# Second products of an attention tile grouped with the scores of the tile two further on

## The chip, the cores and the metric

The program runs on one core of a Trainium2 chip. The metric is the device time of one execution in microseconds (us); each figure in the table below is a whole execution, and the number to be predicted is the median over repeated runs. The engines are PE (matrix products, with PEld for its weight loads), DVE (elementwise), ACT (activations and copies), POOL and SP. In this kernel POOL and SP mostly start DMA transfers, each from a queue that is worked through in order.

## What is computed

Chunked attention, then two feed-forward layers, all in float32:

```python
# q, k, v: batch 8, heads 8, sequence 576, head size 64; chunks of 64
scores = scale * q_c @ k_c.T            # inside each chunk only
attn = softmax(scores)
x = (attn @ v_c)                        # -> 4608 tokens x 512
h = x @ w_in                            # 512 -> 2048
g = maximum(h, 0) + log1p(exp(-abs(h))) # softplus
x = g @ w_out                           # 2048 -> 512
h = maximum(maximum(x @ w1, x @ w2), x @ w3)   # 512 -> 768
out = h @ w_out2                        # 768 -> 512
```

## The kernel before, in words

Tokens are cut into 9 blocks of 512 (`NB`). The attention of a block is 4 tiles (two heads each), 36 tiles in all (`NTILE`). Weights are made of two float32r parts, so a product is three passes. The first three blocks (`NP`) go through `mlp1`: 48 steps, each with 12 matmuls into `ph` and 12 into `acc`. The other six blocks use `UnitA`, seven products a unit in the manner of Strassen, with `mlp1_out`; their weight forms are made in `weightsa`, written to DRAM (`wac`, `wae`) and read back by POOL in `againa`, up to nine slots ahead (`ringa`). The second layer (`Unit2`, `Unit`, `mlp2_out`) follows after some 900 us.

Tiles 0 to 7 are computed by `attention_first`. Tiles 8 to 35 go through `attention(t)`, whose steps are: SP loads q and k (`load_32`, four loads for each piece of the tile), POOL loads v into `rv`, of which there is one buffer (`load_v`); DVE transposes q and k into a slot `QK`; PE computes the scores in the PSUM buffer `aps`, also one; DVE and ACT make the softmax in `p`; DVE transposes it into the slot `PT` in blocks of 32; SP writes it to DRAM (`pd`, L667) and reads it back in four pieces that finish the transposition (L672). PE then multiplies it with v, and `to_x` copies the product out as the layer's input. The products with v of one tile and the scores of another share one `aps` buffer and one PE instruction group, `products` (32 matmuls of 64x64 each). Which two tiles share a group is decided by the list `before`: in the kernel before, group t holds the scores of tile t and the products of tile t-1.

Nobody writes the order of the work by hand. Every piece is an `op` with the engines that may do it, an assumed cost, an assumed extra latency (`lat`) and a due time (`due`). `Plan.order` simulates a list schedule with these assumed numbers, earliest due time first, and hands out buffers and slots as it goes; the order that comes out is each engine's program. On the chip each engine then runs its own list in that order and waits where something isn't there. A step is 6 us in the plan's due times (`STEP`). An operation without a due time gets one by counting back from the operations that need it, their cost and `lat` included.

Slots (46 tiles of 128x2x512) are shared by kind: `w` 32, `x` 8, `z` 4, `qh` 1, `vh` 1. `vh` first holds the signed identities of `conv1`. Raw weights (`conv`) go to `z` or `w`, the last ones to `z` alone; `QK` takes `qh` or `z`; `PT` takes `vh` or `z`.

Of the kernel before, what the change touches and what calls it, by code (L numbers as in the profile page):

```python
# [179 lines left out]
def tile_kernel(ctx: ExitStack, tc: tile.TileContext, q, k, v, w_in, w_out, w1, w2, w3, wo2, out):  # L180
# [71 lines left out]
    def slot(*kinds, shape=[P, 2, TB], dt=F32R):  # L252
        return Buf(*kinds, fresh=lambda i: slot_at(i, shape, dt))
# [26 lines left out]
    NP = 3  # L280
# [179 lines left out]
    def loads(fns, buf, key, move, alloc=(), engs="S", after=(), due=None):  # L460
        fns = list(fns)
        if alloc:
            op({engs: 0.0}, lambda e: None, alloc=alloc, after=after)
        for n, fn in enumerate(fns):
            op(
                {e: 0.5 if due is not None else 0.65 for e in engs},
                lambda e, fn=fn: fn({"A": nc.scalar, "S": nc.sync, "G": nc.gpsimd}[e].dma_start),
                w=[(buf, (key, n))],
                after=after,
                lat=4.0 if due is None else 1.8,  # L470
                move=move / len(fns),
                due=due,
            )
# [140 lines left out]
    def attention(t, after=()):  # L614

        if t < NTILE:
            Rq, Rk, Rv = Buf("rq"), Buf("rk"), Buf("rv")
            QK = slot("qh", "z", dt=F32)
            qT, kT = half(QK, 0), half(QK, 1)
            loads(load_32(t, q, lambda: Rq.t), Rq, "q", 2.2, [Rq], after=after)  # L620
            loads(load_32(t, k, lambda: Rk.t), Rk, "k", 2.2, [Rk], after=after)
            loads(load_v(t, lambda: Rv.t, 0), Rv, "v", 1.6, [Rv], "G", after)
            op({"D": 0.69}, lambda e: nc.vector.transpose(qT(), Rq.t), r=[Rq], w=[(QK, "q")], alloc=[QK])
            op({"D": 0.69}, lambda e: nc.vector.transpose(kT(), Rk.t), r=[Rk], w=[(QK, "k")])
        G = Buf("aps")
        old = before.pop() if before else None

        def products(e):
            if old:
                v4 = old[1].t.rearrange("p (c e d) -> p c e d", e=2, d=D)  # L630
                p4 = old[2].t[:, 1].rearrange("p (a u i) -> p u a i", a=2, i=32)
                for c in range(HP):
                    for r, k in four:
                        at = slice(TB // 2 + c * CH, TB // 2 + (c + 1) * CH)
                        square(G.t[:, :, at], v4[:, c, k], p4[:, k * HP + c], r, k)
            if t < NTILE:
                scores(G, qT, kT)

        parts = [(G, "v")] * (old is not None) + [(G, "s")] * (t < NTILE)
        op(  # L640
            {"P": 0.5 * len(parts) + 0.4},
            products,
            r=([old[1]] + [(old[2], n) for n in range(4)] if old else []) + ([(QK, "q"), (QK, "k")] if t < NTILE else []),
            w=parts,
            alloc=[G],
            after=last_t[-1:],
            due=T0 + STEP * (4 * (t - 1 - HP) + (2.25 if t <= NP * HP else -0.75)),
        )
        if old:

            def view(z, flat):
                if flat:
                    return z.rearrange("p (r f) -> p r f", r=2)
                return z[:, :, TB // 2:]

            to_x(old[0], G, view)
        if t == NTILE:
            return
        pbuf = Buf("p")
        softmax(G, pbuf)  # L660
        PT = slot("vh", "z", dt=F32)
        pt, pT = half(PT, 0), half(PT, 1)
        op({"D": 0.69}, lambda e: nc.vector.transpose(
            pt().rearrange("p (b u i) -> p b u i", b=2, i=32), pbuf.t.rearrange("p (u b i) -> p b u i", b=2, i=32)
        ), r=[pbuf], w=[(PT, "pt")], alloc=[PT])
        pd = Buf("pd")
        op({"S": 0.48}, lambda e: nc.sync.dma_start(out=pd.t, in_=pt()), r=[(PT, "pt")], w=[pd], alloc=[pd], lat=3.0)  # L667
        for n in range(4):
            c, b = divmod(n, 2)
            op(  # L670
                {"S": 0.48},
                lambda e, n=n, c=c, b=b: nc.sync.dma_start(  # L672
                    out=pT()[n * 32:(n + 1) * 32, :].rearrange("j (a f) -> j a f", a=2),
                    in_=pd.t[c * CH:(c + 1) * CH, b * (TB // 2):(b + 1) * (TB // 2)].rearrange("(a j) f -> j a f", a=2),
                ),
                r=[pd],
                w=[(PT, n)],
                lat=4.0,
            )
        before.append((t, Rv, PT))  # L680

# [298 lines left out]

    STAYA = (6, 7)
    EARLY = 4
    GATE = 5
    wa = {}
    began = []

# [419 lines left out]
    def strassen():  # L1406

        groups = [(b, b + 1) for b in range(0, NB - 1, 2)] + [(NB - 1,)]
        units = [("a", b, n) for b in range(NP, NB) for n in range(NJ // 2)]
        units += [("b", i, n) for i in range(len(groups)) for n in range(3 * NJ2 // 2)]  # L1410
        old, outs, side, ready, earlies = None, [], [], [], 0
        for kind, i, n in units + [("", None, 0)]:
            new = None
            if kind == "a":
                at = NJ * i + 2 * n
                t = HP + at // HP
                clock[0] = T0 + STEP * at
                if at % HP == 0 and t <= NTILE:
                    attention(t, [first_loads[11]])
                if n == 0:  # L1420
                    splita(i)
                new = UnitA(i, n, old)
                begin = new.p1()
                if n in (1, 2, 3, 4, 6) and earlies < 4 * NJ2:
                    early(earlies, T0 + STEP * (at + EARLY), [begin])
                    earlies += 1
                if i == NB - 1:
                    mark[n] = begin
            if kind == "b":
                if (i, n) == (0, 0):  # L1430
                    clock[0] = T1
                    for m in range(3 * NJ2 // 2):
                        ready = [weights2(m)]
                    split2(groups[0], [mark[4]])
                new = Unit2(groups[i], n) if i + 1 < len(groups) else Unit(NB - 1, n)
                begin = new.p1()
                if n == 4 and i + 1 < len(groups):
                    if i + 2 < len(groups):
                        split2(groups[i + 1], ready + [begin])
                    else:  # L1440
                        split(NB - 1, [begin])
            if old:
                old.p5()
                old.p4()
            if new:
                new.p6()
            if kind == "a" and outs:
                out_of, *which = outs.pop(0)
                in_line("h", out_of(*which))
            if old:  # L1450
                old.p3()
            if new:
                new.p2()
                new.p7()

            if isinstance(old, UnitA):
                outs += [(mlp1_out, old.b, 2 * old.n + f) for f in (1, 0)]
                pops, least = (1 if kind == "a" else 2), 1
            else:
                pops, least = 2 if len(outs) > 3 else 1, i is None or i + 1 == len(groups)  # L1460
            for _ in range(pops):
                if len(outs) > least:
                    out_of, *which = outs.pop(0)
                    o = out_of(*which)
                    if out_of is mlp1_out:
                        in_line("h", o)
            if isinstance(old, (Unit, Unit2)) and old.i == 2:
                for h, b in enumerate(old.b if isinstance(old, Unit2) else (NB - 1,)):
                    (side if h else outs).extend([(mlp2_out, b, 2 * old.jp + f) for f in range(2)])
                if old.jp == NJ2 // 2 - 1:  # L1470
                    outs, side = outs + side, []
            old = new
        for out_of, *which in outs:
            out_of(*which)
# [24 lines left out]
    for n, (b, j, first, last) in enumerate(steps):  # L1499
        if n >= NJ and n % (NJ // HP) == 0:  # L1500
            t = HP + n // (NJ // HP)
            attention(t, [first_loads[min(t, 11)]])
        h = mlp1(b, j, first, last)
        if b == NP - 1 and j % 2 == 0:
            weightsa(j // 2, [before_last], lead)
        if (b, j) == (1, NJ // 2):
            lead = h
        before_last = h if j % 2 == 0 else before_last
# [38 lines left out]
```

## Time and profile before

| | us |
|---|---|
| runs: median of 3 | 1456.22 |
| runs: lowest, highest | 1453.78, 1457.23 |
| profiled execution, its own time | 1451.92 |
| its span, first to last instruction | 1449.8 |
| mean granted PE clock | 0.987 of full |
| PE busy, share of the span | 97% |
| DVE, ACT, POOL busy | 61%, 35%, 18% |

The profiled execution is one run. Its span starts with the program's first instruction; 2.1 us of its time lie outside. PE's busy time counts matmuls that run at either clock, so a stretch at half clock looks busy. The time line of this program: until 72 us the first tiles and weights, until about 332 us the steps of `mlp1`, until about 900 us the units of `UnitA`, and then the second layer.

### The profile page before, as it was taken

Reading aid. Unit: us, or ns where it says so; the run is one execution under the profiler, and the core shown is the slowest. Engines: PE = TensorE matmul, PEld = TensorE weight load, DVE = VectorE, ACT = ScalarE, POOL = GpSimd, SP = SyncE. Lnnn points to the kernel's source line nnn. Section 1 sums busy time; section 2 is a strip of 40 time slices with the busy share of each in tenths; the row PEclk is TensorE's granted clock in tenths of the full one; section 3 lists DMA queues with packets and bytes.
Section 4 is the critical chain, followed back from the end, with each engine's and each line's share of the span. In section 5 each row is a group of like instructions: output and inputs, shape, how many; then the busy total and the mean of one; then the engine's idle time right before and its main releaser. Section 6 shows DMA issues by size and latency. Waiting matters only on the chain.

```text
span 1449.8 us, 25676 instructions
## 1 busy us (share of the span) xinstructions
PE 1399.2 (97%) x9994; PEld 1200.1 (83%) x9994; DVE 881.6 (61%) x1678; ACT 509.6 (35%) x998; POOL 267.1 (18%) x471
## 2 busy tenths in 40 slices
PE   5999999999899897999998999999999999999998
PEld 4788788888798786888998998888888888888897
DVE  8978866766585575665765457766435444644423
ACT  4533222434344242243343445434213322322212
POOL 1000121332223232323222010211011111101300
PEclk9999999999999998999999999999999999999999
DMA  8554366687867859767567275855344533625720
GB/s 256 172 144 108 110 195 191 181 257 226 263 179 213 263 158 272 216 186 239 178 242 256 101 232 207 302 196 188 119 165 140 206 134 98 232 74 177 294 106 30
DMA packets 232473, 271.99 MB, mean 188 GB/s; under 512 B 143456, under 2 KB 163296, under 8 KB 232352
## 3 DMA queue, kind: packets, MB, share of 16 engines
q0 software_dynamic: 49472, 169.64, 33.4%
q1 hardware_dynamic: 182064, 99.93, 24.5%
q8 instruction: 79, 1.29, 0.4%
q10 hardware_dynamic: 816, 0.79, 0.2%
q14 instruction: 42, 0.34, 0.1%
HBM read 208.14 MB, written 62.13 MB: 186 GB/s over the span
## 4 chain that ended last, share of the span: by engine, by line
PE 85%; DMA 7%; issue 3%; DVE 3%; POOL 1%; SPq 1%; ACT 1%; DVEq 0%; ACTq 0%; POOLq 0%
PE ph L1279 14%; PE acc L1176 13%; PE ph L1102 12%; PE acc L1387 10%; PE one L1279 10%; PE acc L737 9%; PE ph L717 9%; DMA s<-pd 3%; PE aps L486 2%; DMA pd<-s 2%; PE ph L970 2%; PE one L970 1%; PE acc L486 1%; PE ph L388 1%; POOL rv L453 1%
## 5 line engine op out<-in xcount | busy, mean ns | idle before, releaser
L1176 PE MATMUL acc<-g,s 128*128 128x512 f32 x1152 | 284.4, 396 | 0.0
L1102 PEld LDWEIGHTS ph<-s,s 128*128 128x128 f32 x2016 | 256.3, 193 | 10.2 <-ACT tmp L1124 2.1
L1102 PE MATMUL ph<-s,s 128*128 128x256 f32 x2016 | 261.4, 285 | 1.4 <-ACT tmp L1124 1.2
L1176 PEld LDWEIGHTS acc<-g,s 128*128 128x128 f32 x1152 | 213.5, 191 | 41.8
L266 ACT COPY tmp<-ph 128x256 f32<-128x256 f32 (+1 forms) x271 | 123.2, 454 | 349.4 <-PE ph L1279 218.7
L1279 PE MATMUL ph<-s,s 128*128 128x512 f32 x864 | 212.6, 389 | 0.0
L273 DVE TENSOR_TENSOR tmp<-one,tmp 128x512 f32<-128x512 f32 (+1 forms) x123 | 77.8, 632 | 211.8 <-PE one L1279 173.2
L1279 PEld LDWEIGHTS ph<-s,s 128*128 128x128 f32 x864 | 162.2, 188 | 33.6
L453 POOL DMA_DIRECT2D rv<-in_v_dram x152 | 93.6, 623 | 359.8 <-PE aps L486 306.9
L1279 PE MATMUL one<-s,s 128*128 128x512 f32 x648 | 158.8, 389 | 0.0
L273 DVE TENSOR_TENSOR g<-tmp,g 128x512 fp32r<-128x512 f32 x168 | 115.0, 686 | 65.8 <-ACT g L266 65.2
L273 DVE TENSOR_TENSOR tmp<-ph,tmp 128x256 f32<-128x256 f32 (+1 forms) x172 | 76.5, 455 | 114.8 <-PE ph L1102 114.6
L1279 PEld LDWEIGHTS one<-s,s 128*128 128x128 f32 x648 | 121.5, 188 | 25.0
L737 PE MATMUL acc<-g,s 128*128 128x512 f32 x576 | 140.2, 392 | 0.0
L717 PE MATMUL ph<-s,s 128*128 128x512 f32 x576 | 139.4, 392 | 0.0
L717 PEld LDWEIGHTS ph<-s,s 128*128 128x128 f32 x576 | 109.0, 190 | 23.0
L737 PEld LDWEIGHTS acc<-g,s 128*128 128x128 f32 x576 | 107.1, 188 | 23.0 <-DVE g L273 0.3
L844 POOL DMA_DIRECT2D s<-w2c x96 | 51.1, 533 | 354.2 <-PE one L1279 130.5
L266 ACT CAST g<-tmp 128x512 fp32r<-128x512 f32 x163 | 101.6, 623 | 39.4 <-PE acc L737 18.6
L1124 ACT ACTIVATE tmp<-tmp 128x256 f32<-128x256 f32 x96 | 50.4, 525 | 148.6 <-DVE tmp L273 148.6
L266 ACT CAST s<-tmp 128x512 fp32r<-128x512 f32 (+1 forms) x122 | 72.0, 601 | 62.9 <-DVE tmp L273 42.0
L1039 POOL DMA_DIRECT2D s<-wac x108 | 59.2, 549 | 166.0 <-PE ph L1102 139.6
(134 smaller groups left out, 1511.8 us busy)
## 6 DMA issues: line engine op xcount, KB each, us to landing
s<-wac POOLq DMA_DIRECT2D x108, 512.0 KB, 5.5
s<-w2c POOLq DMA_DIRECT2D x96, 512.0 KB, 4.6
w2c<-s POOLq DMA_DIRECT2D x24, 512.0 KB, 4.2
wac<-s POOLq DMA_DIRECT2D x18, 512.0 KB, 4.3
x2d<-tmp SPq DMA_DIRECT2D x36, 256.0 KB, 3.7
s<-wae POOLq DMA_DIRECT2D x18, 512.0 KB, 6.5
s<-in_moe_w_dram POOLq DMA_DIRECT2D x18, 512.0 KB, 5.1
s<-in_moe_w_in_dram SPq DMA_DIRECT2D x16, 512.0 KB, 4.6
```

Source lines behind the costliest of these rows:

```text
L266: nc.scalar.copy(dst(), src())
L273: return op({"D": 0.69 * n}, lambda e: nc.vector.tensor_tensor(dst(), a(), b(), f), r=r, w=w, **kw)
L453: dma(out=dst().rearrange("p (c e d) -> p c e d", e=2, d=D)[half * CH:(half + 1) * CH, lo:lo + mine, h, :], in_=v[b, t % HP * 2 + h].rearr ...
L717: nc.tensor.matmul(ph.t, w[:, wi, kk * P:(kk + 1) * P], x[kk].t[:, xi], start=(kk == 0 and wi == 0 and xi == 0), stop=(kk == KD - 1 and wi ...
L737: nc.tensor.matmul(acc[m // 2].t[:, m % 2], w[:, wi, m * P:(m + 1) * P], g.t[:, gi, :], start=(first and wi == 0 and gi == 0), stop=(last ...
L844: lambda e, k=k, z=z, w=w: nc.gpsimd.dma_start(out=z.t[:, :, w].bitcast(F32), in_=(w2e[n // 2] if k == 3 else w2c[n][k])[:, :, w]),
L1039: lambda e, k=k: nc.gpsimd.dma_start(out=new[k].t.bitcast(F32), in_=wac[n][k] if k < 3 else wae[n // 2]),
L1102: nc.tensor.matmul(z.t[:, half * HT:(half + 1) * HT], ws.t[:, wi, col + kk * P:col + (kk + 1) * P], x.t[:, xi, kk * HT:(kk + 1) * HT], sta ...
L1124: in_line("y", op({"A": n}, lambda e: nc.scalar.activation(to(), src(), AF.Softplus), r=r, w=w))
L1176: nc.tensor.matmul(acc[m // 2].t[:, m % 2], w.t[:, wi, m * P:(m + 1) * P], g.t[:, gi, :], start=(first and wi == 0 and gi == 0), stop=(las ...
L1279: nc.tensor.matmul(dst(), ws.t[:, wi, col + kk * P:col + (kk + 1) * P], x[kk].t[:, xi], start=(first and kk == 0 and wi == 0 and xi == 0), ...
L1387: nc.tensor.matmul(acc[t // 2].t[:, t % 2], g.t[:, gi, t * P:(t + 1) * P], wo.t[:, wi], start=(j == 0 and wi == 0 and gi == 0), stop=(j == ...
```

## The change

Group t now holds the scores of tile t and the products of tile t-2. So that products come out at the same place of the loops, every tile's `attention` call stands one tile earlier (two calls at the first place), and there are two last groups without scores. The due time of the groups is given by a new formula, the assumed latencies of the loads, of the write to `pd` and of the reads back are raised, `PT` may also take a slot of kind `w`, and the reads back of `wac` are let go one `weightsa` earlier (`GATE`).

```diff
@@ loads
-                lat=4.0 if due is None else 1.8,
+                lat=5.0 if due is None else 1.8,
@@ attention
-        old = before.pop() if before else None
+        old = before.pop(0) if len(before) == 2 or t >= NTILE else None
...
-            due=T0 + STEP * (4 * (t - 1 - HP) + (2.25 if t <= NP * HP else -0.75)),
+            due=T0 + STEP * (13.0 + 3.56 * (t - 2 * HP) if t <= 4 * HP else 4 * t - 23.0),
...
-        if t == NTILE:
+        if t >= NTILE:
             return
...
-        PT = slot("vh", "z", dt=F32)
+        PT = slot("vh", "z", "w", dt=F32)
...
-        op({"S": 0.48}, lambda e: nc.sync.dma_start(out=pd.t, in_=pt()), r=[(PT, "pt")], w=[pd], alloc=[pd], lat=3.0)
+        op({"S": 0.48}, lambda e: nc.sync.dma_start(out=pd.t, in_=pt()), r=[(PT, "pt")], w=[pd], alloc=[pd], lat=8.0)
...
-                lat=4.0,
+                lat=8.0,
@@ strassen and the steps of mlp1
-    GATE = 5
+    GATE = 4
...
-                t = HP + at // HP
+                t = HP + at // HP + 1
...
-                if at % HP == 0 and t <= NTILE:
+                if at % HP == 0 and t <= NTILE + 1:
...
-            attention(t, [first_loads[min(t, 11)]])
+            for t in ((t, t + 1) if n == NJ else (t + 1,)):
+                attention(t, [first_loads[min(t, 11)]])
```

## Rows read from the trace of the kernel before

**Rows 1.** The page: span; busy time and share of PE and others.

```profile
span 1449.8 us, 25676 instructions
PE 1399.2 (97%) x9994; PEld 1200.1 (83%) x9994; DVE 881.6 (61%) x1678; ACT 509.6 (35%) x998; POOL 267.1 (18%) x471
```

**Rows 2.** PE's waits, 126 to 800 us: total, times, longest.

```profile
PE aps L486 <- DMA s<-pd: 27.0, 12, 8.0
PE ph L388 <- DVE s L345: 1.5, 1, 1.5
```

**Rows 3.** A window: length, busy time by engine, PE clock, DMA share, GB/s.

```profile
800.00:1365.00 565.00, 565.00 (x2701) 476.45 (x2700) 302.74 (x509) 193.98 (x364) 77.76 (x145) 1.00 0.49 174
```

**Rows 4.** Windows of PE alone at half clock: two of five, and their sum.

```profile
391.23:398.05 6.82, 5.49 (x71) 0.50 0.69 191
...
572.13:582.37 10.24, 4.35 (x69) 0.50 0.86 237
...
sum 27.29, PE 20.07; mean PE 4.01
```

**Rows 5.** Windows, one from a block's first unit to the next block's.

```profile
526.70:631.10 104.40, 93.42 (x849) 83.58 (x848) 67.66 (x135) 36.66 (x80) 32.53 (x54) 0.95 0.76 217
631.10:721.30 90.20, 89.61 (x786) 80.58 (x785) 56.36 (x112) 35.45 (x77) 26.12 (x44) 1.00 0.72 215
```

**Rows 6.** The chain that ended last, 366 to 396 us: start, length, what.

```profile
377.46 6.58 DMA pd<-s
...
384.96 7.43 DMA s<-pd
...
392.53 0.44 PE aps L486 x2
```

**Rows 7.** Time lines of PE and SP, 545 to 583 us: one tile's trip.

```profile
549.60 0.65 PE L486 MATMUL aps<-s 64*64 64x64 f32 x32
...
576.67 0.44 PE L486 MATMUL aps<-s,rv 64*64 64x64 f32 x2 [7.95 <-DMA s<-pd]
578.46 1.02 PE L486 MATMUL aps<-s,rv 64*64 64x64 f32 x27 [1.35 <-DMA s<-pd]
...
558.31 0.37 SPq L667 DMA_DIRECT2D pd<-s  x1
...
562.86 6.35 SPq L672 DMA_DIRECT2D s<-pd  x4
```

**Rows 8.** Loads of v, 320 to 800 us (ns min/median/max); PE's and POOL's time lines.

```profile
L453 POOL DMA_DIRECT2D rv<-in_v_dram x104: 534/628/922, 324.1 to 774.8; - x104
...
DMA to landing us min/median/max: 1.8/2.4/6.3
...
650.00 0.65 PE L486 MATMUL aps<-s 64*64 64x64 f32 x32
...
657.17 3.06 POOL L453 DMA_DIRECT2D rv<-in_v_dram  x5 [4.58 <-issue]
```

**Rows 9.** Windows of the weight stage, columns as in rows 3.

```profile
150.00:170.00 20.00, 20.00 (x148) 16.43 (x147) 17.98 (x38) 5.69 (x11) 3.73 (x6) 1.00 0.48 159
170.00:190.00 20.00, 18.53 (x95) 14.56 (x97) 15.28 (x31) 6.70 (x13) 0.00 (x0) 1.00 0.26 72
```

**Rows 10.** Time lines of PE, ACT and DVE, 156 to 212 us.

```profile
158.83 0.69 PE L486 MATMUL aps<-s,rv 64*64 64x64 f32 x32
...
189.74 0.69 PE L486 MATMUL aps<-s,rv 64*64 64x64 f32 x32
...
185.04 0.58 ACT L266 CAST s<-aps 128x512 fp32r<-128x512 f32 x1
...
183.73 0.70 DVE L624 STREAM_TRANSPOSE s<-rk 128x512 f32<-128x512 f32 x1
```

**Rows 11.** Reads back of the weight forms (L1039), 320 to 900 us.

```profile
  PE ph L1102: 161.8, 43
...
DMA to landing us min/median/max: 3.4/5.4/10.6
```

## The prediction, made before any run

> **What bounds the kernel now.** Read first the page's busy times: PE is busy for 97% of the span and no other engine for more than 83% [rows 1], so a change is worth what it does to PE. The 1449.8 us of span less 1399.2 us of PE leave 50.6 us idle. Then read PE's waits: between 126 and 800 us it waits 27.0 us in 12 pieces for the transfer that brings the transposed softmax back from `pd`, and next to nothing for anything else [rows 2]. From 800 us on a window shows PE busy for all of its 565 us [rows 3], so the second layer holds nothing to win, and the first 126 us hold work of `attention_first` that the change leaves alone. Then read the clock: five stretches, each beginning at or soon after such a wait, ran at half of the granted clock (1.2 instead of 2.4 GHz). In their 27.29 us PE was busy for 20.07 [rows 4]; at full clock that work takes half, so 10.0 us are lost there. Together the waits cost 37.0 us.
>
> A second way to the same number is to compare blocks. The block that starts at 631 us has no such wait and takes 90.20 us; the one at 526.7 us takes 104.40 with 93.42 busy, that is 11 us idle and 3.8 us of work at the slow clock [rows 5]. Same work, 14.2 us apart.
>
> Why does PE wait? Follow one tile. The scores end at 550.2 us, the softmax reaches SP as a write at 558.31, the four reads back are issued over 6.35 us from 562.86, and PE can begin the products only at 576.67, after 7.95 us idle and with another piece still missing [rows 7]. That is 26 us from scores to products. The chain shows where such a trip goes elsewhere: 6.58 us for the write and 7.43 us for the last read, which ends just before PE's products at 392.53 [rows 6]. In the kernel before the products of tile t-1 stand in the group of tile t, so one trip must fit between two groups, which are four steps apart: 90.20 / 4 = 22.5 us [rows 5]. A trip of 18 to 22 us costs nothing and one of 26 us stalls all of PE, since the products stand in front of the next matmuls in PE's list.
>
> **The change, part by part.**
>
> The distance of two. Products of tile t-2 stand in the group of tile t, so a trip has two spacings, 45 us. The longest trip I found is the one above; its last piece lets PE go on at 578.46, 28 us after the scores [rows 7]. The spare is then 17 us. The waits of 27.0 us go, and with them the 10.0 us at the slow clock, since each of those stretches follows such a wait. What is late next at a group: v, q and k, or the copy-out.
>
> v. There is still one `rv`. It comes free with the products of tile t-1 (now in group t+1) and is needed in group t+2, one spacing as before. After the group that ends at 650.65 us the last five of its loads are issued from 657.17 to 660.23 and land 2.4 us (median) to 6.3 us (most) later, so at 662.6 to 666.5 [rows 8]: 12 to 16 us of the 22.5. Spare 6 us or more; cost 0.
>
> q and k. The scores now come earlier against the rest: one tile at the call, and more by the due times. Sixteen loads on SP and two transposes on DVE move with them, and the five SP transfers of the trip too. The shortest lead I found in the trace is 6 us, the second transpose at 183.73 for the group at 189.74 [rows 10], and it comes of the same hold: that group was waiting for `aps`, whose product with v (158.83) could be copied out only at 185.04 [rows 10], because slots for x were taken. With the distance of two the first products come one group later, so group 9 no longer holds `aps`. I take 0; bounds -2 to +3 us.
>
> The weight stage. Until about 190 us DVE also splits the weights, and is busy 17.98 of 20 us and 15.28 of 20 us [rows 9]. One more tile before that time brings seven DVE passes of about 0.70 us [rows 10], 4.9 us, against 2.0 + 4.7 = 6.7 us idle. PE waits there once already, 1.5 us for a weight [rows 2]. If all of it fits the cost is 0, if none of it does 4.9 us, plus half of a slow-clock stretch as in the sum above (2 us, a fifth of 10.0). I take 2 us.
>
> Slots. `PT` now lives over two spacings, so about two are alive instead of one; the second takes a slot of `z`, or of `w`. Weights' raw loads of the last rows need `z`, and the reads back of `wac` take what is free. They land 5.4 us (median) to 10.6 us (most) after issue, and POOL's own wait ahead of them is mostly for PE to free a slot, 161.8 us in 43 waits [rows 11]; so slots do set when they start. But PE has no wait for them in its list [rows 2], so the lead of up to nine slots covers them now, and one slot fewer takes a ninth of that lead. The lower bound is 0, the upper one such transfer in full view of PE, 10.6 us; I take 1 us, near the row that shows no wait.
>
> One group more. There are now 30 groups instead of 29, since the first two have no products and the last two no scores. No matmul is added. The start of one more group costs between 0 and the 0.65 us that a whole half group of 32 matmuls takes [rows 7]; I take 0.3 us.
>
> The due times, the assumed latencies and `GATE` cost no instruction. They shift where SP, DVE and POOL take up work. The larger latencies place the reads back of `pd` later in SP's list, with other loads between, so SP stands less in front of them; as two spacings are there, that later place costs nothing up to 17 us. `GATE` lets nine reads of 512 KB go two steps earlier, into a time where DMA has room (share 0.72 to 0.76 in the busier blocks [rows 5]); 0, bounds -1 to +2.
>
> Products' place. `to_x` feeds the layer. By the formulas a group is due three steps (some 17 us) before its block starts instead of 4.75, but in the trace groups run late on their due times because each waits in the plan for the trip before it. With that gone they come on time, so I cost this at 0.
>
> The sum, against the profiled execution's own 1451.92 us: less 27.0, less 10.0, plus 0.3, plus 2, plus 1, gives 1418.2. The median of the runs lies 4.3 us above the profiled execution. These waits hang on transfers and so differ from run to run, and I put at least half of the 4.3 us down to them; with them gone the difference shrinks to about 2. Forecast 1420.
>
> **A rule that speaks against it.** The loads of v are issued by POOL at 534 to 922 ns each, 628 at the median [rows 8], beside a DVE that is busy for two thirds of the time [rows 5]. The Trainium skill, page SBUF — State Buffer, section "A bandwidth-pool intuition that's wrong (but worth ruling out)", says that a DMA issued from GpSimd that takes about 620 ns alone takes about 3100 ns beside a DVE copy that locks the shared port. By that rule six loads would take 18.6 us and v would miss its 22.5 us in a denser block. The trace does not agree so far: none of 104 issues took a microsecond.
>
> **The rivals.**
>
> A: part is given back. Slots or DVE make weights late at 160 to 190 us, or some trips or loads still end after their group in the densest blocks (DMA share 0.76 [rows 5] becomes 0.88 when 104.4 us shrink to 90.2). Price: the upper bounds above, 6.9 + 10.6 + 3 + 2 = 22 us instead of 3.3, so up to 1438; typical 1429. For it: POOL waits for slots, and DVE is full. Against it: PE shows no wait for either now.
>
> B: it does not do what it says. If the reads back come so late in SP's list that the trip takes two spacings too, the waits stay: 1450 to 1458. This needs 17 us more than the longest trip seen.
>
> C: v becomes the bound, and the kernel is slower. v's trip has one spacing before and after. From 22.5 us on, each of some 20 groups between 330 and 800 us waits for the excess, and half a slow-clock stretch comes with most of them (2 us). To eat the 37 us gained takes 1.9 us at each of 20 groups, clock included, so the change turns slower where v needs about 24 us from group to landing. At 26 us the price is 20 x (3.5 + 2) = 110 us less the 37: about 1527. Against it: 12 to 16 us now. For it: the loads stand behind POOL's waits for slots, in a list whose order is new.
>
> **How the numbers follow.** Forecast (waits and slow clock gone, little given back, 1412 to 1425): 0.64. A (1425 to 1440): 0.25. B: 0.04. C: 0.05. Something else small: 0.02. The low end is the sum with nothing given back and a gain at q and k (1451.92 - 37.0 + 0.3 - 2 = 1413), the high end is A at its upper bound. The range 1412 to 1438 holds about 0.86 of this by my count; I keep it so wide for the unknown costs. A measurement of this kernel can tell about 0.2% (3 us) from no change. Faster by more: forecast and A and a share of the rest, 0.91. Same: most of B, 0.03. Slower: C and a rest, 0.06.
>
> **What would show it.** In PE's waits the row for `pd` should be gone or below 3 us, and the mean granted clock should rise from 0.987 to about 0.995. Blocks should all take 89 to 92 us. SP's reads back should be complete 15 us or more before their group. A new wait of PE for `rv`, for a weight slot (`wac`) or for L345 would be A or C. The second layer's length, from 900 us to the end, should not move. I would be wrong if the order that the plan makes moves something that this trace does not show as short, for example the splitting of x before a block's first unit.

## The result, and the profile after

| | before | after |
|---|---|---|
| runs: median (lowest, highest) of 4 | 1455.0 (1452.84, 1457.23) | 1433.2 (1427.58, 1437.47) |
| profiled execution, its own time | 1451.92 | 1433.25 |
| its span | 1449.8 | 1431.5 |
| mean granted PE clock | 0.987 | 0.991 |

The ratio is 0.985, 95% interval 0.981 to 0.989: 22 us faster, where 35 to 36 were forecast. The time lies in the range given, at the place of rival A.

The windows show where it happened. Each of the next two lines is the stretch from the first unit of `UnitA` to the first unit of its last block, in before and in after; the columns are as in [rows 3].

```profile
332.30:814.30 482.00, 453.48 (x3859) 406.49 (x3858) 305.91 (x613) 180.82 (x393) 136.11 (x229) 0.97 0.71 218
```

```profile
335.20:796.50 461.30, 446.69 (x3828) 400.11 (x3827) 306.99 (x615) 178.47 (x396) 136.22 (x231) 0.99 0.73 227
```

The stretch became 20.7 us shorter. PE begins it 2.9 us later, and from its end to the end of the span 635.5 us became 635.0: the whole gain is here, and the second layer didn't move.

PE's waits in after, 126 to 800 us, against [rows 2]:

```profile
PE ph L1102 <- DVE tmp L273: 6.2, 7, 2.0
PE ph L1102 <- ACT tmp L266: 4.4, 2, 2.5
PE ph L1102 <- ACT tmp L1124: 3.8, 6, 0.8
PE ph L388 <- DVE s L345: 1.5, 1, 1.5
```

The row for `pd` is gone: 27.0 us of it went to nothing. In its place stand 14.4 us at L1102, the first product of a unit step, which waits for DVE or ACT to empty its PSUM buffer `ph`. In before these were 1.4 us:

```profile
PE ph L1102 <- ACT tmp L1124: 1.2, 2, 0.6
PE ph L1102 <- ACT tmp L266: 0.2, 1, 0.2
```

The half-clock windows after 126 us, against [rows 4], are two instead of five:

```profile
464.52:467.93 3.41, 3.41 (x10) 0.50 0.91 323
505.48:508.89 3.41, 3.38 (x14) 0.50 1.04 332
sum 6.82, PE 6.79; mean PE 3.39
```

So the old cost of 37.0 us (27.0 and 10.0) went, and 13.0 + 3.4 us came back as waits for DVE and ACT and the slow clock that goes with them. That leaves 20.6 of the 20.7 us.

Who keeps DVE and ACT? DVE's own waits, 330 to 800 us, first in after and then in before (total, times, longest):

```profile
DVE tmp L317 <- DMA s<-in_moe_w_dram: 41.2, 16, 5.2
...
DVE tmp L317 <- DMA s<-in_moe_w_out_dram: 8.6, 3, 3.9
```

```profile
DVE tmp L317 <- DMA s<-in_moe_w_dram: 16.5, 7, 5.9
...
DVE tmp L317 <- DMA s<-in_moe_w_out_dram: 1.9, 1, 1.9
```

L317 is the first operation of `conv`, here called by `early`: while `UnitA` runs, the second layer's raw weights are loaded by POOL and split by DVE, 24 of them. Only the second layer needs them, from some 900 us on. But DVE's list is in order, and when L317 stands in front of a load that hasn't landed, what empties `ph` stands behind it. One such place in after, by the time line of all engines:

```profile
498.69 0.77 POOL L303 DMA_DIRECT2D s<-in_moe_w_dram  x1 [4.46 <-PE ph L1102]
...
504.70 0.43 DVE L317 TENSOR_SCALAR tmp<-s 128x512 int32<-128x512 int32 x1 [3.81 <-DMA s<-in_moe_w_dram]
...
505.04 0.42 DVE L273 TENSOR_TENSOR tmp<-ph,tmp 128x256 f32<-128x256 f32 x1
...
505.51 2.72 PE L1102 MATMUL ph<-s,s 128*128 128x256 f32 x11 [2.04 <-DVE tmp L273]
```

POOL issues the load at 498.69, DVE stands still for 3.81 us until 504.70, does one operation, empties `ph` at 505.04, and PE goes on at 505.51 after 2.04 us idle, at half clock. The row of PE's wait names DVE L273; what DVE itself stood in front of is the load in the first row. That load was also issued late: POOL had stood 4.46 us for PE just before it.

The plan counts 4.0 us from the issue of such a load to its landing (1.0 before the move, 2.2 for the move, 0.8 after it). Measured from the issue to the landing for the loads of L303 (18 of the 24; the other six are those of L308), 330 to 800 us, in before and in after:

```profile
DMA to landing us min/median/max: 4.1/5.1/7.9
```

```profile
DMA to landing us min/median/max: 4.5/5.8/9.3
```

Taken load by load in after: had each landed 4.0 us after its issue, 35.0 of DVE's 49.8 us (41.2 and 8.6) would be gone (an estimate from the issue, the landing and DVE's wait of each). The other 14.8 us are loads that were issued late for their place in DVE's list. Of the 3.81 us above, 2.0 are the one and 1.8 the other.

### The profile page after: what moved, and what is told of

Its sections match the earlier page's. It is cut to its first block, busy times and chain, and to the rows that moved or that the text cites. A ratio compares the mean times of both kernels' runs of the same rounds, so it can differ in the third digit from the quotient of the medians.

```text
span 1431.5 us, 25706 instructions
## 1 busy us (share of the span) xinstructions
PE 1394.8 (97%) x9994; PEld 1194.9 (83%) x9994; DVE 883.0 (62%) x1676; ACT 507.1 (35%) x1000; POOL 266.4 (19%) x471
## 4 chain that ended last, share of the span: by engine, by line
PE 85%; DMA 8%; DVE 3%; issue 2%; POOL 1%; SPq 1%; ACT 1%; ACTq 0%; POOLq 0%
PE ph L1279 14%; PE acc L1176 12%; PE ph L1102 12%; PE acc L1387 10%; PE one L1279 10%; PE ph L717 9%; PE acc L737 9%; DMA s<-in_moe_w_dram 2%; PE aps L486 2%; PE ph L970 2%; DMA pd<-s 2%; PE one L970 1%; PE acc L486 1%; DMA rq<-in_q_dram 1%; DMA s<-pd 1%
## 5 line engine op out<-in xcount | busy, mean ns | idle before, releaser
L1176 PE MATMUL acc<-g,s 128*128 128x512 f32 x1152 | 281.3, 393 | 0.2 <-DVE g L273 0.2
L1102 PE MATMUL ph<-s,s 128*128 128x256 f32 x2016 | 264.8, 285 | 14.4 <-DVE tmp L273 6.2
L1102 PEld LDWEIGHTS ph<-s,s 128*128 128x128 f32 x2016 | 256.6, 192 | 26.5 <-DVE tmp L273 7.6
L1176 PEld LDWEIGHTS acc<-g,s 128*128 128x128 f32 x1152 | 211.9, 190 | 40.8 <-DVE g L273 0.5
L273 DVE TENSOR_TENSOR tmp<-one,tmp 128x512 f32<-128x512 f32 (+1 forms) x122 | 77.1, 632 | 211.7 <-PE one L1279 173.3
L273 DVE TENSOR_TENSOR g<-tmp,g 128x512 fp32r<-128x512 f32 x168 | 115.3, 686 | 77.7 <-ACT g L266 77.2
L717 PE MATMUL ph<-s,s 128*128 128x512 f32 x576 | 140.1, 393 | 0.3 <-DVE s L273 0.3
L273 DVE TENSOR_TENSOR tmp<-ph,tmp 128x256 f32<-128x256 f32 (+1 forms) x172 | 76.1, 454 | 86.2 <-PE ph L1102 85.6
L717 PEld LDWEIGHTS ph<-s,s 128*128 128x128 f32 x576 | 108.7, 190 | 23.7 <-DVE s L273 0.8
L1039 POOL DMA_DIRECT2D s<-wac x108 | 58.4, 542 | 158.9 <-PE ph L1102 115.4
```

The costliest lines, as they stand in the source:

```text
L273: return op({"D": 0.69 * n}, lambda e: nc.vector.tensor_tensor(dst(), a(), b(), f), r=r, w=w, **kw)
L717: nc.tensor.matmul(ph.t, w[:, wi, kk * P:(kk + 1) * P], x[kk].t[:, xi], start=(kk == 0 and wi == 0 and xi == 0), stop=(kk == KD - 1 and wi ...
L1039: lambda e, k=k: nc.gpsimd.dma_start(out=new[k].t.bitcast(F32), in_=wac[n][k] if k < 3 else wae[n // 2]),
L1102: nc.tensor.matmul(z.t[:, half * HT:(half + 1) * HT], ws.t[:, wi, col + kk * P:col + (kk + 1) * P], x.t[:, xi, kk * HT:(kk + 1) * HT], sta ...
L1176: nc.tensor.matmul(acc[m // 2].t[:, m % 2], w.t[:, wi, m * P:(m + 1) * P], g.t[:, gi, :], start=(first and wi == 0 and gi == 0), stop=(las ...
```

## The experiments

Theory 1: PE's new waits come of transfers that land later than the plan assumes, with DVE or ACT standing in front of them in order; first of all the raw loads. Theory 2: PE, DVE and the transfers are simply fuller per us, and some 10 to 15 us come back in any case. A third question is which part of the change carries the gain.

**raw_not_read.** The lists of PE, ACT, POOL and SP are those of the changed kernel, instruction for instruction, and DVE's has the same operations in the same order. Only the operand of three of them in each conversion differs: they read a constant that is already in SBUF instead of the raw weights that POOL loads, so the second layer's products are taken with other weights. The first of the three stands for all:

```diff
-        hw = lambda: raw.t[:, :, 1]
-        lw = lambda: raw.t[:, :, 0]
+        still = lambda s: ident.bitcast(I32).rearrange("p (n s) -> p s n", s=2)[:, s][:, None, :].to_broadcast([P, 8, 64]); v8 = lambda x: x.rearrange("p (n s) -> p n s", n=8) if by == "G" else x
+        hw, lw = lambda: still(1) if by == "G" else raw.t[:, :, 1], lambda: still(0) if by == "G" else raw.t[:, :, 0]
...
-            lambda e: nc.vector.tensor_scalar(ai(), hw(), 0x7FFFFFFF, None, ALU.bitwise_and),
+            lambda e: nc.vector.tensor_scalar(v8(ai()), hw(), 0x7FFFFFFF, None, ALU.bitwise_and),
```

> The changed kernel with every engine's list as it is; only the three DVE operations of the early conversions read a small constant tile instead of the raw weights that POOL loads, so that DVE doesn't wait for those loads (the loads still run; the second layer's weights are therefore wrong, the work is the same). Theory 1, DVE stands in front of raw loads that land later than the plan assumes, and PE's new waits in UnitA come of that: DVE's wait for these loads goes from 50 us to 0, PE's waits at L1102 from 14.4 us to under 5, both half-clock stretches may go, time 1418 to 1424. Theory 2, the rest is given back because DVE and the transfers are simply fuller per us now that PE doesn't stall: PE's waits at L1102 stay at 10 us or more, time 1430 to 1436.

Measured: 1417.5 us (1417.2 to 1425.6), ratio to before 0.976 (0.973 to 0.980). PE's waits, 126 to 800 us, and the stretch of `UnitA`:

```profile
PE ph L1102 <- ACT tmp L1124: 3.2, 2, 2.7
PE ph L388 <- DVE s L345: 1.5, 1, 1.5
```

```profile
335.10:780.10 445.00, 441.58 (x3827) 397.75 (x3826) 307.34 (x615) 179.03 (x396) 136.48 (x231) 1.00 0.75 235
```

The same order without these reads is 15.7 us faster, with DVE as busy (307.34 against 306.99 us in a shorter stretch) and as many bytes moved in less time (235 against 227 GB/s). Theory 2 falls: fuller engines did no harm. The edit takes away a second dependence as well: POOL no longer waits until DVE has read a raw weight before it loads the next (24.6 and 7.0 us ahead of the loads of L303 and L308 in after). That the gain doesn't come of this is seen in all_lats2 below, which still has 23.1 us of it and is as fast.

And 482.0 less 445.0 is 37.0 us, the forecast's sum for the pd waits and their clock. That it fits to the tenth is luck: PE's idle time in the stretch fell by 25.1 us (28.52 to 3.42) and its busy time by 11.9 (453.48 to 441.58), where the sum has 27.0 and 10.0.

**before_not_read.** The same edit, with the same constant for weights, on the kernel before.

> The kernel before with every list as it is, and the early conversions reading the constant tile instead of the raw weights (which are loaded all the same; the second layer's weights are wrong by that). If the raw loads hold PE up only once the pd waits are gone: 1448 to 1456, PE's waits for pd stay at 20 us or more. If they were part of the pd waits already (DVE late, so the softmax late): 1435 to 1447, waits for pd under 18 us.

Measured: 1449.6 us (10 runs), ratio 0.996 (0.994 to 0.998).

```profile
PE aps L486 <- DMA s<-pd: 21.8, 10, 6.3
PE ph L388 <- DVE s L345: 1.5, 1, 1.5
```

The first expectation held, though the waits for `pd` fell too, from 27.0 to 21.8 us. Four us in before against 15.7 in after: the raw loads cost little as long as PE was held up by `pd`, and without that a wait for them takes the place of the one removed. That need not all have been hidden before: DVE's waits for these loads grew as well, from 18.4 us to 49.8. How much of that growth comes of the new order, and how much of a PE that no longer stalls, no run tells apart.

**early_lat6.** The plan is told that the load takes longer.

```diff
-        in_line("load", op({by: 0.5}, load, w=[raw], alloc=[free, raw], after=after, lat=2.0, move=2.2, due=first))
+        in_line("load", op({by: 0.5}, load, w=[raw], alloc=[free, raw], after=after, lat=2.0 if by == "S" else 6.0, move=2.2, due=first))
```

> The changed kernel; the plan assumes 6.0 us instead of 2.0 us of latency for the raw loads that POOL issues. Theory 1: the plan puts other DVE work ahead of each conversion, DVE's wait for these loads falls from 50 us to under 15, PE's waits at L1102 to under 7, time 1418 to 1426. Theory 2: time 1430 to 1436, as only the order of equal work changes.

Measured: 1429.8 us (1428.1 to 1431.4), above what theory 1 said and just under what theory 2 said. PE's waits at L1102 are 9.7 us, not under 7. DVE's wait for the raw loads did fall, to 8.7 us in the row for `w_out` and some 2 us besides (50 in after), but PE has two large waits left, and the time line of the largest shows two others of the same kind:

```profile
632.74 0.71 DVE L623 STREAM_TRANSPOSE s<-rq 128x512 f32<-128x512 f32 x1 [4.12 <-DMA rq<-in_q_dram]
...
637.05 0.37 ACT L266 COPY tmp<-ph 128x256 f32<-128x256 f32 x1 [7.99 <-DMA x2d<-tmp]
...
637.48 1.65 PE L1102 MATMUL ph<-s,s 128*128 128x256 f32 x6 [4.71 <-ACT tmp L266]
```

DVE stands in front of q for 4.12 us, and ACT for 7.99 us in front of a `tmp` buffer whose store of x (L705) hasn't landed. So theory 1 was right about DVE's wait for the raw loads and wrong about the time; it may have named too few of the transfers. Whether this is so, or whether any new order brings its own 10 us, is asked by the next two.

**all_lats** and **all_lats2.** Longer assumed latencies for all of them.

```text
# lat of:            changed  all_lats  all_lats2
# raw loads (POOL)     2.0      6.0       8.0
# loads of q, k, v     5.0      9.0       9.0
# stores of x          2.5      6.0       9.0
# stores to w2d        2.0      6.0       9.0
# stores to wo2d       2.0      6.0      10.0
```

> The changed kernel with longer assumed latencies for every transfer that DVE or ACT was seen to stand in front of: 6.0 for the raw loads of POOL, 9.0 for the loads of q, k and v, 6.0 for the stores of x, of the second layer's weights and of its split. If PE's remaining waits come of transfers that land later than the plan assumes, with whichever transfer is the shortest in the plan: PE's waits at L1102 under 6 us, no or one half-clock stretch after 330 us, 1416 to 1424. If early_lat6 failed to gain because any new order brings about 10 us of waits, whatever it assumes: 1426 to 1434.

Measured: 1426.1 us (1424.0 to 1429.8), the lower end of the second expectation, with two half-clock stretches after 330 us where none or one were expected. PE's waits at L1102 did fall under 6 us (4.8). The two waits of 3 us and more that are left (3.6 at L1102, 3.0 at L1176) both follow stores of the second layer's weights (`wo2d`) that hold up ACT for 8.1 us and DVE for 5.4.

> As all_lats, with 8.0 for raw loads, 9.0 for the stores of x and of the second layer's weights, 10.0 for those of its split. all_lats was left with two waits of over 3 us behind stores of that split that had not landed; if these go, 1416 to 1423. If they only move elsewhere: 1424 to 1432.

Measured: 1414.9 us (1412.6 to 1419.1), ratio to before 0.974 (0.972 to 0.977), with PE's waits in 126 to 800 us

```profile
PE ph L1102 <- ACT tmp L266: 1.5, 1, 1.5
PE ph L388 <- DVE s L345: 1.5, 1, 1.5
PE ph L1102 <- ACT tmp L1124: 0.7, 2, 0.5
```

and the stretch of `UnitA` at full clock:

```profile
335.90:779.60 443.70, 441.46 (x3828) 397.72 (x3827) 307.52 (x613) 178.21 (x395) 135.00 (x230) 1.00 0.76 236
```

This is 18 us faster than the changed kernel and some 39 than the one before, just under the first expectation, and it differs from the changed one in assumed latencies alone. Three quarters of the distance from 1429.8 to here came with the step from all_lats to all_lats2, in which the stores of x, w2d and wo2d and the raw loads all grew; which of the four it was, no run tells apart.

**dist_only** and **all_lats_dist.** The distance of two and the earlier calls on the kernel before, with its latencies, kinds of slot and `GATE`; the due time is the old one for the tile whose products are in the group. all_lats_dist adds the latencies of all_lats.

```diff
-            due=T0 + STEP * (4 * (t - 1 - HP) + (2.25 if t <= NP * HP else -0.75)),
+            due=T0 + STEP * (4 * (t - 2 - HP) + (2.25 if t <= NP * HP + 1 else -0.75)),
```

> The kernel before with the distance of two and the calls one tile sooner, but with the old latencies, the old kinds of slot for PT, GATE 5, and the old due times counted for the tile whose products are in the group. If the distance is what removes the waits: PE waits under 3 us for the reads back of pd (27.0 before), and the time is 1420 to 1440, according to what other waits the new order has. If the latencies and due times do the work: waits for pd of 10 us or more, 1440 to 1455.

Measured: 1427.7 us (1423.9 to 1428.7), no PE wait for `pd`. The distance alone carries the whole gain; this is even faster than the full change, with its waits for raw loads at 26.6 instead of 41.2 us in the row of L317.

> The distance alone with the longer assumed latencies of all_lats. 1418 to 1428 if these two add up (1427.7 and the 7 us that all_lats gained on the changed kernel), 1426 to 1434 if a new order brings new waits.

Measured: 1419.0 us (1417.8 to 1419.9). The two add up, and the order is another one than that of all_lats2: the gain doesn't hang on one lucky order.

**old_lats** and **old_due.** The changed kernel with the old latencies, and with the due times of dist_only.

> The changed kernel with the old assumed latencies (4.0 for loads, 3.0 and 4.0 for the trip through pd). If the distance carries the gain: within 8 us of the changed kernel, 1425 to 1441, waits for pd under 3 us. If the latencies do: 1445 to 1455 with waits for pd back.

Measured: 1447.3 us (1442.4 to 1449.3), the time of the second expectation without its waits. PE's waits, 126 to 800 us (of the profiled execution, 1442.4, the fastest of the five):

```profile
PE ph L1102 <- ACT tmp L266: 11.9, 4, 5.6
PE ph L1102 <- DVE tmp L273: 6.1, 4, 4.9
PE aps L486 <- DMA s<-pd: 2.3, 1, 2.3
```

The waits for `pd` do stay away with the distance, as the first half of the expectation said. The time is bad for another reason: the row for ACT, whose own waits have 20.8 us for the landing of the stores of x. Of the 37 us that the distance takes off, some 29 are lost again. PE's two longest waits, 5.6 and 4.9 us, have ACT in front of a store of x (7.1 us) and DVE in front of a raw load (6.3 us) ahead of them.

> The changed kernel with the old due times counted for the tile whose products are in the group, which differs from the distance alone (1427.7) in latencies, the slot kind w and GATE. If the new due times cost something: 1420 to 1430. If what differs between these kernels is only which transfers happen to be late for their list: 1425 to 1440, with some 10 us of waits at L1102 behind loads, whatever the due times.

Measured: 1437.3 us (1436.2 to 1439.0), 4 us above the changed kernel, whose runs overlap with these, with 11.1 us of PE behind ACT at L1102. With the new latencies, then, no cost of the new due times is seen. With the old latencies two kernels that differ in the due times, the slots `w` and `GATE` lie 20 us apart (dist_only 1427.7, old_lats 1447.3); which of the three does it, or only the order that came out, no run tells apart.

**lat_only.** The kernel before with the change's three latencies and nothing else.

> The kernel before with the raised latencies of the change alone (5.0 for loads, 8.0 and 8.0 for the trip), products one group behind their scores as before. A trip is then about 25 us in the plan against a spacing of 22.5, so the plan itself puts the groups further apart: PE's waits for pd fall below 10 us, but the last tile of a block comes late and PE waits for x at a block's start; 1455 to 1490. If the latencies are what the change needed: 1420 to 1440.

Measured: 1539.7 us (1538.4 to 1544.6), ratio 1.060. More waiting for `pd`, not less:

```profile
PE aps L486 <- DMA s<-pd: 68.4, 14, 13.5
PE ph L1102 <- ACT s L266: 15.3, 6, 2.7
```

At a distance of one the trip paces the plan: a longer assumed trip moves every group back, until the last tile of a block is what PE stands in front of: 14 waits at seven groups, every fourth one, the longest of 13.5 us, and six more of up to 2.7 us behind ACT's copies for x. The expectation had the direction and missed that `pd` itself would be the wait, and the size by 50 us. Without the distance, the latencies of the change cost some 86 us.

**gate5** and **no_w.** `GATE` back to 5; `PT` without the slots `w`.

> The changed kernel with the reads back of wac let go at the old place. If GATE matters little, as forecast: 1428 to 1438, within 5 us of the changed kernel. If the earlier reads gave a part of the gain or of the loss: outside that.

> The changed kernel with PT in vh or z only. If slots for PT bind: weights or the reads back of wac come late, PE waits 5 us or more for them, 1438 to 1450. If they don't bind: 1427 to 1438.

Measured: 1435.5 us (1433.4 to 1437.4) and 1436.9 us (1432.6 to 1439.2), against 1427.6 to 1437.5 for the changed kernel. Neither can be told from it. In gate5 PE waited twice for v, 2.0 us in all, the only such wait in any of these runs.

## Why the prediction was right or wrong

**The waits for pd: right.** The distance takes the whole row away, in every kernel with the distance but old_lats, which keeps 2.3 us. With the raw loads out of the way the stretch of `UnitA` is 37.0 us shorter, the forecast's sum, by luck to the tenth.

**The clock: right in kind.** Each half-clock stretch after 126 us in before began during a wait for `pd` or within 2 us of its end, and they went with these waits; the two that are in after go with waits at L1102 of 2.54 and 2.04 us. The mean of 0.995 that was forecast was nearly reached without those (0.994 in raw_not_read and all_lats2). The forecast left out a stretch at half clock in the first 42 us, which was 10.24 us long in before and 17.07 in after.

**What is late next: the step that failed.** The prediction asked "what is late next at a group: v, q and k, or the copy-out" and looked, besides the groups, at the weight stage, the slots and one more group. What was late next stood at none of these. It was DVE in front of raw weights, for operations whose results nobody needs before the second layer. The rows gave a warning: DVE's waits in before had 16.5 and 1.9 us for these loads, which became 41.2 and 8.6. I read PE's waits, found 1.4 us for L1102, and took that for a small term, though what the wait to be removed hides now has to be looked for in the waits of the engines behind PE. The terms for what is given back came to 3.3 us; measured, the raw loads alone are 15.7.

**v: right.** No wait in after. The loads of v against [rows 8]:

```profile
L453 POOL DMA_DIRECT2D rv<-in_v_dram x104: 534/623/918, 321.5 to 764.4; - x104
...
DMA to landing us min/median/max: 1.8/3.1/7.0
```

Landing took 0.7 us longer at the median, well inside the spare of 6 us. The rule that spoke against it, from the Trainium skill, page SBUF — State Buffer, section "A bandwidth-pool intuition that's wrong (but worth ruling out)", that such a DMA takes about 3100 ns beside a DVE copy that locks the shared port, isn't what this trace shows either: DVE was busy for 307 of 461 us, and the longest of 104 issues took 918 ns. No DVE operation between 320 and 800 us took longer than 0.71 us, so what a longer copy would do isn't shown. Rival C is out.

**q and k, one group more:** within their bounds as far as can be seen. One of the waits at L1102 (2.54 us) has DVE in front of k for 2.47 us before it, and ACT in front of a store of x for 5.58, as in early_lat6.

**The weight stage: 2 us taken, 0 found.** The one wait of 1.5 us at L388 is the same in before and after. PE reaches the first unit of `UnitA` 2.9 us later, but 1.5 us of that are there at the first product of `mlp1` already (L717 starts at 36.74 us in before and at 38.21 in after), ahead of the weight stage. Some 0.7 us more is the half group that now stands ahead of the units; the rest is not explained.

**Slots and GATE: 1 us and 0 taken, nothing measurable found** (no_w, gate5). That POOL waits long for slots [rows 11] was true, and PE has no wait for a weight slot in after. Ahead of a raw load such a wait is not free, as the 4.46 us at 498.69 us show.

**SP's reads back: this sign didn't hold.** "Complete 15 us or more before their group" fails for 13 of the 28 tiles. With longer assumed latencies the plan lets the reads go later, 8.6 us after the write at the median, against 4.5 in before and 4.9 in old_lats. The four of one tile were issued from 395.46 and the last landed at 402.8, for a group at 408.50.

```profile
395.46 2.07 SPq L672 DMA_DIRECT2D s<-pd  x4
...
408.50 0.69 PE L486 MATMUL aps<-s,rv 64*64 64x64 f32 x32
```

The second spacing is thus partly used up by choice, and 5.7 us of spare are left at this tile, the least of the 28. It was enough.

**Blocks of 89 to 92 us:** four of five in after, by the first product of each block; the other took 97.4 and has both of the half-clock stretches.

**The rivals.** A came true in its time and hardly in its reasons: it named weights late at 160 to 190 us and trips or loads that end after their group, and neither gave anything back that can be seen. That the range held the time is luck in this sense. What gave some 16 us back is a mechanism that A doesn't have, loads that are late for DVE's list; late issues behind POOL's waits are a smaller part of it. B and C didn't happen. A chance of 0.64 for the likeliest case was bold for a sum whose "what is late next" was looked up on one engine.

**The median against the profiled execution:** 3.1 us apart in before (4.3 by the three runs known at the forecast), 0.05 in after. The forecast's guess that this difference hangs on the waits for `pd` fits, but one profiled execution of each can't show it.

## What to carry to other kernels

When a wait of the busiest engine is to be removed, read the waits of the engines that feed and empty it, and ask of each wait for a transfer what stands behind it in that engine's list: an operation that nobody needs yet can hold up the one that everybody needs. In a list made by a plan, the assumed latency of a transfer helps to decide this. Here it paid to assume more for all the transfers that DVE and ACT had stood in front of, urgent or not (1433.2 to 1414.9 us), while the same on the path that paces the plan cost (lat_only, 1539.7). To tell a hidden wait from mere load, keep every list as it is and take away the dependence alone, by letting the operation read data that is already there.

## What the runs showed of the hardware that was not expected

A load of 512 KB by POOL lands 5.1 us after its issue at the median while the core moves 218 GB/s, 5.8 at 227, with 9.3 us as the longest. The Trainium skill, page DMA: Bandwidth & Descriptors, section "Anatomy of one DMA — SWDGE (gpsimd) path", gives 2.0 us plus the bytes at 436 GB/s for such a transfer, which would be 3.2 us for this one (an estimate from that page). The runs here are above that by 1.9 and 2.6 us at the median. The share of the other transfers in this isn't shown: no run here times such a load alone, and all_lats2, with 236 GB/s, has 5.7 us. The plan's own 4.0 us are short by 1.1 and 1.8 us at the median, and by 5.3 at most.
